# Batch 1's pooling in a fused attention and MoE kernel: plain loads and narrow matmuls in place of accumulating loads

## Chip, cores, metric

One core of one Trainium2 chip. The metric is device time in microseconds (us), the median of several executions. Ratios are the mean time of one kernel's fast runs over that of the other's fast runs of the same rounds, so they are not quite the ratio of the medians quoted beside them.

## What is computed

```python
# q: 4 x 12288 x 128   kv: 4 x 384 x 32 x 128   w_sr: 128 x 128
kv_pool = kv.reshape(B, H//4, 4, W//4, 4, C).mean(axis=(2, 4))    # 4 x 4 pixels -> 1: 768 rows a batch
k = v = kv_pool.reshape(B, -1, C) @ w_sr
a = softmax(q @ k.T / sqrt(C));  x = (a @ v).reshape(49152, 128)
h = x @ moe_w_in                                                  # 128 -> 2048
out = (h * sigmoid(1.702 * h)) @ moe_w_out                        # 2048 -> 128
```

## The kernel before

The work is cut into 96 groups of 512 queries; batch 1 begins at group 24. A **chunk** is 128 keys (attention) or 128 hidden units (MoE) for one group. A **tile** is up to three chunks: TensorE fills three PSUM banks (the fill), ScalarE (ACT) takes them in one activation and writes them to a ring of 108 chunk slots, and TensorE later uses each slot (12 value matmuls empty three attention chunks). Groups 0 to 47 go through attention, then through the MoE; then 48 to 95. A scheduler in the program places all this in one fixed order per engine. The parts that matter:

```python
def load_chunk(b, jc):              # batch 0 only: 1 MB of pixels, cast to bf16, into a free part of x
    a, ch = divmod(jc, HC)
    t = x_tile(XS - 1 - jc)
    nc.gpsimd.dma_start(out=t, in_=kv_r[b, a, ch])
    ...
def pool_chunk(b, jc):              # 16 matmuls of 32 columns sum the pixels
    ...
def add_kv(b, n):                   # batches 1 to 3: 16 loads, the later 14 ADD into what has landed
    i, w = divmod(n, r)
    if n == 0:
        kv_sums[b] = kvsum.tile([Hp, 2, Wp, C], F32, name="kvs")
    for i2 in range(2):
        nc.gpsimd.dma_start(out=kv_sums[b][:, i2], in_=kv_p[b, i, w, :, i2],
                            **({"accum_op": ADD} if n else {}))

def cast_q(s):                      # 2048 queries: f32 in DRAM -> bf16 in DRAM, GpSimd's queue
    nc.gpsimd.dma_start(out=q_bf[sl, :].rearrange("(p i) c -> p (i c)", p=128), in_=...)

def load_qT(s):                     # the same queries, transposed by the DMA, SP's queue
    qTs[s] = qpool.tile([128, 1, SG], BF, name="qT")            # three buffers
    nc.sync.dma_start_transpose(out=qTs[s], in_=q_bf[s * SG:(s + 1) * SG, :])

ADDS = [4, 6, 8, 9, 11, 12, 14, 15]
def background(i):                  # called when group i's first fill is placed
    s = i // 4
    if i % 4 == 0:
        if QS <= s + 2 < NS:
            load_qT(s + 2)          # first at i = 8: the queries of groups 16 to 19
        if CAST <= s + CAST < NS:
            cast_q(s + CAST)        # three tiles further ahead
    if i in ADDS:
        add_kv(1, ADDS.index(i))
    if i in (17, 19):
        use_kv(1, (i - 17) // 2)
    ...                             # i == 26 and 34: the two MoE weights
```

GpSimd's order of issue does not follow TensorE: it issues the next load as soon as that load's own waits are met. The queries of groups 0 to 15 are loaded directly and transposed on TensorE; the DMA transposes begin with those of group 16.

The softmax here doesn't subtract the row's maximum and nothing guards it: scores larger than these inputs give would overflow.

Of the kernel before, what the change touches and what calls it, by code (L numbers as in the profile page):

```python
# [20 lines left out]
def kernel(  # L21
    ctx, tc, q, kv, w_sr, moe_w_in, moe_w_out, out,
):
    nc = tc.nc
    B, N, C = q.shape
# [4 lines left out]
    JC = J // 128  # L30
# [9 lines left out]
    K = 3  # L40
# [37 lines left out]
    def acc(key=None):  # L78

        nonlocal last_acc  # L80
        last_acc = next_acc()
        if key:
            closes[last_acc] = key
        return banks[:, last_acc, :]

    def next_acc():
        return min((m for m in (13 - last_acc, last_acc) if m not in closes), key=lambda m: free[m])
# [12 lines left out]
    def x_tile(s):  # L100
        return x[:, s % XS * SG:(s % XS + 1) * SG]
# [5 lines left out]
    kv_tiles, kv_sums, pooled, pTs, kTs, vs = {}, {}, {}, {}, {}, {}  # L107

    def new_keys(b):
        kTs[b] = kvres.tile([128, J], BF, name="kT")  # L110

        vs[b] = kvres.tile([128, JC, C + 2], BF, name="v")
        nc.vector.memset(vs[b][:, :, C:C + 1], 1.0)

    def load_chunk(b, jc):
# [4 lines that stand above are left out]
        kv_tiles[b, jc] = t.rearrange("p (wp w1 c) -> p w1 wp c", w1=r, c=C)  # L120
# [19 lines left out]
    def value_chunk(b, jc):  # L140
        ps = acc()
        nc.tensor.matmul(ps[:, 0:128], pTs.pop((b, jc)), w_sr_sb, start=True, stop=True)
        nc.vector.tensor_copy(vs[b][:, jc, 0:C], ps[:, 0:128])


    def add_kv(b, n):
# [7 lines that stand above are left out]
    def sum_kv(b, a):  # L154
        t = kv_sums[b][:, :, 4 * a:4 * a + 4, :]
        pooled[b, a] = kvtmp.tile([Hp, 4, C], BF, name="pooled")
        nc.vector.tensor_tensor(pooled[b, a], t[:, 0], t[:, 1], ADD)  # L157
# [25 lines left out]
    def cast_q(s):  # L183
        sl = slice(s * SG, (s + 1) * SG)
        nc.gpsimd.dma_start(out=q_bf[sl, :].rearrange("(p i) c -> p (i c)", p=128),  # L185
                            in_=q_flat[sl, :].rearrange("(p i) c -> p (i c)", p=128))

    def load_qT(s):
        qTs[s] = qpool.tile([128, 1, SG], BF, name="qT")
        nc.sync.dma_start_transpose(out=qTs[s], in_=q_bf[s * SG:(s + 1) * SG, :])  # L190
# [58 lines left out]
    w_sr_sb = cpool.tile([128, C], BF)  # L249
# [46 lines left out]
    def room_ahead():  # L296
        busy = set(slot_of.values())
        return next((n for n in range(AG) if (head + n) % AG in busy), AG)
# [45 lines left out]
        nc.vector.tensor_copy(x[:, o:o + n * T], ps.rearrange("p k t -> p (k t)"))  # L344

    av_of, xt_of, turns = {}, {}, []
    ADDS = [4, 6, 8, 9, 11, 12, 14, 15]
    CAST = 5

    def background(i):  # L350
# [4 lines that stand above are left out]
                load_qT(s + 2)  # L355
            if CAST <= s + CAST < NS:
                cast_q(s + CAST)
        if i in ADDS:
            add_kv(1, ADDS.index(i))
        if i in (17, 19):  # L360
            use_kv(1, (i - 17) // 2)
        if i == 26:
            nc.gpsimd.dma_start(out=w_in_sb, in_=moe_w_in)
        if i == 34:
            nc.gpsimd.dma_start(out=w_out_sb, in_=moe_w_out.rearrange("(o p) c -> p o c", p=128))
# [9 lines left out]
    def use_kv(b, a):  # L375
        sum_kv(b, a)
        extras.extend([(transpose_pooled, b, a), (make_k, b, a), (make_v, b, a)])

    extras = []
# [55 lines left out]
    def prepare(p):  # L435
# [10 lines left out]
        for i, _ in part:  # L446
# [5 lines left out]
        0: [(pool_chunk, 0, 0), (warm, 2), (key_chunk, 0, 0), (warm, 2)],  # L452
        1: [(transpose_q, 1), (transpose_q, 2), (transpose_q, 3), (warm, 3)],
        2: [(pool_chunk, 0, 1), (value_chunk, 0, 0), (warm, 2), (key_chunk, 0, 1)],
        4: [(transpose_q, 4), (transpose_q, 5), (transpose_q, 6)],
        5: [(transpose_q, 7)],
        6: [(pool_chunk, 0, 2), (value_chunk, 0, 1)],
        8: [(key_chunk, 0, 2)],
        9: [(pool_chunk, 0, 3), (value_chunk, 0, 2)],
        11: [(key_chunk, 0, 3)],  # L460
        12: [(pool_chunk, 0, 4), (value_chunk, 0, 3)],
# [10 lines left out]

    FIXED, CHUNK, SWITCH, HANDOVER, EVACUATE, LATE = 0.33, 1.975, 6.0, 1.0, 4.5, 1.0
    COST = {pool_chunk: (2.5, 2.0), key_chunk: (0.7, 2.0), value_chunk: (0.7, 2.0),
            transpose_q: (1.2, 4.0),
            transpose_pooled: (1.5, 3.0), make_k: (1.0, 3.0), make_v: (1.5, 3.0), turn: (1.5, 3.5)}
    SMALL, TURN = 0.27, 5.5
    PAUSE = 4.0
    now, end, extra_at = 0.0, [], 0.0
    done = 0  # L480

    def fill(p):
        nonlocal now
        if p >= len(seq):
            return
        kind, part = seq[p]
        prepare(p)
        lo = K * (p % 2)
        (fill_attn if kind == "a" else fill_moe)(part, banks[:, lo:lo + len(part), :])
        if p >= 2:  # L490
            now = max(now, end[p - 2] + HANDOVER / 2)
        now += len(part)
        begin = max(now + HANDOVER / 2, end[p - 1] if p else 0.0)
        if p and kind != seq[p - 1][0]:
            begin += SWITCH
        end.append(begin + FIXED + CHUNK * len(part))
# [3 lines left out]
    for n in range(len(seq)):  # L500
        fill(n + 2)
        while True:
            room = room_ahead()
            limit = end[-1] - K - HANDOVER if n + 3 < len(seq) else 1e9
            bank = free[next_acc()]
            f = None
            if turns and max(now, bank) >= turns[0][0]:
                f, args = turn, turns[0][1:]
            if f is None and extras and now >= max(extra_at, bank):
                f, *args = extras[0]  # L510
            if f and max(now, bank) + COST[f][0] > limit + (LATE if f is turn else 3 * LATE) and room >= 4 * K:
                f = None
            if f:
                now = max(now, bank) + COST[f][0]
                f(*args)
                free[last_acc] = now + COST[f][1]
                extra_at = now + PAUSE
                if f is turn:
                    turns.pop(0)
                else:  # L520
                    extras.pop(0)
                continue
            if done == len(todo):
                break
            kind, i, c = todo[done]
            needs = at[("at" if kind == "a" else kind, i, c)]
            cost = K * SMALL if kind == "a" else 1.0
            if needs > n or (kind == "a" and i % TS == c == 0 and at["at", i + TS - 1, 1] > n):
                break
            start = max(now, end[needs] + HANDOVER)  # L530
            if c == 0 and (kind == "m" or i % TS == 0):
                start = max(start, bank)
            if start + cost > limit and not (room < 2 * K + 1 or (room < 4 * K and start == now)):
                break
            now = start + cost
            (drain_attn if kind == "a" else drain_moe)(i, c)
            done += 1
# [31 lines left out]
```

## Time and profile before

| | before |
|---|---|
| time, median (range) | 1021.14 us (1019.84 to 1021.26) |
| span in the profile | 1019.1 us |
| ACT busy; idle before softmax activations | 957.1 us (94%); 49.1 us |
| longest single wait of ACT | 36.0 us |

ACT is full from 104 us to the end. The lines, and how they are read, are in the prediction below.

### The profile page before, as it was taken

The numbers are of one execution on the slowest core, as the hardware profiler recorded it, in microseconds if no ns is written. First come the engines' busy times: TensorE is split into PE (matmuls) and PEld (weight loads), VectorE is DVE, ScalarE is ACT, GpSimd is POOL, SyncE is SP. The second block draws the span as 40 slices with busy tenths as digits, with TensorE's granted clock in tenths as the row PEclk, the third lists the DMA queues.
The fourth block names the chain that finished last, engine by engine and source line by source line (L and its number), as shares of the span: only waits on it lengthen the run. The fifth ranks groups of instructions, "written<-read, shape, count | busy, mean of one in ns | idle before, by whom it ended". The sixth has DMA issues, their size and how long they took to land.

```text
span 1019.1 us, 15867 instructions
## 1 busy us (share of the span) xinstructions
PE 961.4 (94%) x6461; PEld 525.2 (52%) x6579; DVE 228.1 (22%) x498; ACT 957.1 (94%) x713; POOL 79.3 (8%) x85
## 2 busy tenths in 40 slices
PE   7841999999999999999999999999999999999997
PEld 3530677774444444444445777775444444444443
DVE  4420444441111011101112444442011111011111
ACT  4950999999999999999999999999999999999996
POOL 4224123100023200000000000000000000000000
PEclk9985999999999999999999999999999999999999
DMA  9999999402269952222234121000222222222223
GB/s 181 194 139 149 189 161 159 55 2 32 42 102 159 185 103 39 34 41 42 42 57 79 42 63 42 2 2 11 42 42 42 38 36 41 42 42 42 39 36 50
DMA packets 284009, 72.42 MB, mean 71 GB/s; under 512 B 247712, under 2 KB 282144, under 8 KB 283616
## 3 DMA queue, kind: packets, MB, share of 16 engines
q0 software_dynamic: 39440, 35.66, 24.6%
q1 hardware_dynamic: 243440, 35.61, 22.2%
q8 instruction: 51, 0.84, 0.4%
q10 hardware_dynamic: 1056, 0.13, 0.1%
q14 instruction: 22, 0.18, 0.1%
HBM read 52.49 MB, written 35.65 MB: 86 GB/s over the span
## 4 chain that ended last, share of the span: by engine, by line
PE 85%; DMA 8%; ACT 3%; issue 2%; POOL 1%; DVE 1%; SPq 0%; POOLq 0%; DVEq 0%
PE banks L386 31%; PE banks L393 31%; PE banks L320 12%; PE banks L309 10%; DMA kvs<-in_kv_dram 6%; ACT ag L388 3%; PE banks L342 2%; DMA x<-in_kv_dram 2%; POOL kvs L151 0%; POOL x L197 0%; DMA out_dram<-o_sb 0%; POOL x L119 0%; DVE o_sb L400 0%; PE banks L162 0%; POOL q_bf L185 0%
## 5 line engine op out<-in xcount | busy, mean ns | idle before, releaser
L388 ACT ACTIVATE ag<-banks 128x1536 bf16<-128x1536 f32 x512 | 690.6, 1474 | 0.2
L386 PE MATMUL banks<-x,w_in_sb 128*128 128x512 bf16 x1489 | 412.4, 379 | 2.8 <-ACT ag L388 0.3
L393 PE MATMUL banks<-ag,w_out_sb 128*128 128x512 bf16 x1509 | 406.6, 379 | 1.4
L311 ACT ACTIVATE ag<-banks 128x1536 bf16<-128x1536 f32 (+2 forms) x196 | 260.7, 1457 | 49.1 <-PE banks L309 48.7
L393 PEld LDWEIGHTS <-w_out_sb 128*128 128x128 bf16 x1536 | 150.0, 98 | 179.3
L386 PEld LDWEIGHTS <-w_in_sb 128*128 128x128 bf16 x1536 | 147.7, 98 | 168.2 <-issue 2.3
L400 DVE STREAM_TRANSPOSE o_sb<-banks 128x512 f32<-128x512 f32 x96 | 68.7, 716 | 537.8 <-PE banks L393 509.2
L320 PEld LDWEIGHTS <-ag 128*128 128x128 bf16 x2304 | 152.2, 98 | 50.5 <-issue 2.3
L320 PE MATMUL banks<-v,ag 128*128 128x129 bf16 x2304 | 173.8, 220 | 0.3 <-DVE x L344 0.3
L309 PE MATMUL banks<-qT,kT 128*128 128x512 bf16 x532 | 154.7, 381 | 8.0 <-ACT ag L311 4.5
L151 POOL DMA_DIRECT2D kvs<-in_kv_dram x48 | 60.3, 1262 | 249.0 <-DMA kvs<-in_kv_dram 135.2
L331 DVE TENSOR_TENSOR xt<-banks,rec 128x384 bf16<-128x384 f32 x128 | 71.3, 557 | 4.4
L309 PEld LDWEIGHTS <-kT 128*128 128x128 bf16 x576 | 49.3, 97 | 34.5 <-issue 4.4
L344 DVE COPY x<-banks 128x768 bf16<-128x768 bf16 x64 | 35.6, 557 | 64.2 <-PE banks L342 64.2
L328 DVE RECIPROCAL rec<-banks 128x3 f32<-128x3 f32 x128 | 22.8, 178 | 97.4 <-PE banks L320 97.4
L162 PE MATMUL banks<-ident,pooled 96*128 96x96 bf16 x24 | 2.2, 217 | 35.6 <-DVE pooled L157 35.6
L342 PE MATMUL banks<-ident,xt 128*128 128x128 bf16 x384 | 31.8, 218 | 0.0
L342 PEld LDWEIGHTS <-xt 128*128 128x128 bf16 x384 | 24.8, 97 | 3.3
L162 PEld LDWEIGHTS <-pooled 96*128 96x128 bf16 x24 | 1.6, 102 | 37.3 <-DVE pooled L157 36.3
L185 POOL DMA_DIRECT2D q_bf<-in_q_dram x20 | 13.1, 912 | 11.9 <-DMA q_bf<-in_q_dram 5.3
L157 DVE TENSOR_TENSOR pooled<-kvs 96x512 bf16<-96x512 f32 x6 | 3.9, 658 | 35.0 <-DMA kvs<-in_kv_dram 35.0
L214 DVE COPY qT<-banks 128x512 bf16<-128x512 bf16 x15 | 9.8, 687 | 4.9 <-PE banks L208 4.8
(47 smaller groups left out, 72.5 us busy)
## 6 DMA issues: line engine op xcount, KB each, us to landing
out_dram<-o_sb SPq DMA_DIRECT2D x382, 64.0 KB, 2.0
kvs<-in_kv_dram POOLq DMA_DIRECT2D x48, 384.0 KB, 6.8
q_bf<-in_q_dram POOLq DMA_DIRECT2D x20, 512.0 KB, 18.0
x<-in_kv_dram POOLq DMA_DIRECT2D x6, 512.0 KB, 14.4
x<-in_q_dram POOLq DMA_DIRECT2D x3, 512.0 KB, 20.8
w_in_sb<-in_moe_w_in_dram POOLq DMA_DIRECT2D x1, 512.0 KB, 15.1
w_out_sb<-in_moe_w_out_dram POOLq DMA_DIRECT2D x1, 512.0 KB, 26.0
x<-in_q_dram POOLq DMA_DIRECT2D x1, 384.0 KB, 7.4
```

What stands on the lines that cost most here:

```text
L151: nc.gpsimd.dma_start(out=kv_sums[b][:, i2], in_=kv_p[b, i, w, :, i2], **({"accum_op": ADD} if n else {}))
L309: nc.tensor.matmul(ps[:, k, :], kTs[i // GB][:, jc * 128:(jc + 1) * 128], rhs, start=True, stop=True)
L311: nc.scalar.activation(place([("a",) + c for c in chunks]), ps, AF.Exp, scale=scale)
L320: nc.tensor.matmul(av_of[u][:, k * (C + 1):(k + 1) * (C + 1)], weights(("a", i, jc))[:, o:o + T], vs[i // GB][:, jc, 0:C + 1], start=(jc = ...
L328: nc.vector.reciprocal(rec, ps[:, :, C])
L331: nc.vector.tensor_tensor(xt_of[u // 2][:, u % 2 * TS:u % 2 * TS + TS, :], ps[:, :, 0:C], rec.unsqueeze(2).broadcast_to([128, TS, C]), MUL)
L342: nc.tensor.transpose(ps[:, k, :], xt[:, k, :], ident)
L344: nc.vector.tensor_copy(x[:, o:o + n * T], ps.rearrange("p k t -> p (k t)"))
L386: nc.tensor.matmul(ps[:, k, :], w_in_sb[:, fc * 128:(fc + 1) * 128], x[:, g % (4 * XS) * G:(g % (4 * XS) + 1) * G], start=True, stop=True)
L388: nc.scalar.activation(place([("m",) + c for c in chunks]), ps, AF.Gelu_apprx_sigmoid)
L393: nc.tensor.matmul(o_of[g], w_out_sb[:, fc, :], weights(("m", g, fc)), start=(fc == 0), stop=(fc == FCH - 1))
L400: nc.vector.transpose(o_sb, o_of.pop(g))
```

## The change

The intent: batch 1 no longer hangs on a chain of 16 loads each waiting for another. Its pixels are loaded by six plain loads at group 9, pooled by narrow matmuls as batch 0's are, and a chunk's key and value rows are made in one PSUM bank. The whole diff:

```diff
+    def key_and_value(b, jc):
+        if jc == 0:
+            new_keys(b)
+        ps = acc()
+        nc.tensor.matmul(ps[:, 0:128], w_sr_sb, pTs[b, jc], start=True, stop=True)
+        nc.tensor.matmul(ps[:, 128:256], pTs.pop((b, jc)), w_sr_sb, start=True, stop=True)
+        nc.vector.tensor_copy(kTs[b][:, jc * 128:jc * 128 + 128], ps[:, 0:128])
+        nc.vector.tensor_copy(vs[b][:, jc, 0:C], ps[:, 128:256])
@@
-    ADDS = [4, 6, 8, 9, 11, 12, 14, 15]
@@ background(i)
-        if i in ADDS:
-            add_kv(1, ADDS.index(i))
-        if i in (17, 19):
-            use_kv(1, (i - 17) // 2)
+        if i == 9:
+            for jc in range(JC):
+                load_chunk(1, jc)
+        if 0 <= i - 16 < JC:
+            extras.append((key_and_value, 1, i - 16))
+        if 0 <= i - 15 < JC:
+            extras.append((pool_chunk, 1, i - 15))
@@ scheduler
-            transpose_q: (1.2, 4.0),
+            transpose_q: (1.2, 4.0), key_and_value: (1.0, 3.0),
@@
-            if f and max(now, bank) + COST[f][0] > limit + (LATE if f is turn else 3 * LATE) and room >= 4 * K:
+            if f and max(now, bank) + COST[f][0] > limit + (LATE if f is turn else 4.5) and room >= 4 * K:
```

## The prediction

> **What bounds the kernel now.** I read the page first, for the engine that is busiest and the time at which it is not.
>
> ```profile
> PE   7841999999999999999999999999999999999997
> ACT  4950999999999999999999999999999999999996
> PEclk9985999999999999999999999999999999999999
> DMA  9999999402269952222234121000222222222223
> ...
> L388 ACT ACTIVATE ag<-banks 128x1536 bf16<-128x1536 f32 x512 | 690.6, 1474 | 0.2
> L311 ACT ACTIVATE ag<-banks 128x1536 bf16<-128x1536 f32 (+2 forms) x196 | 260.7, 1457 | 49.1 <-PE banks L309 48.7
> ```
>
> Each slice is 25.5 us. From the fifth on ScalarE (ACT) and TensorE (PE) are both full, and ACT's gate is exact: 0.2 us of idle time before 512 activations of the gelu, 49.1 us before the 196 of the softmax. So ACT sets the pace everywhere except in the first four slices, where the fourth digit is 0 on ACT and 1 on PE. The waits say what that hole is, and ACT's timeline says how long.
>
> ```profile
> ACT ag L311 <- PE banks L309: 48.7, 14, 36.0
> DVE pooled L157 <- DMA kvs<-in_kv_dram: 35.0, 1, 35.0
> PE banks L162 <- DVE pooled L157: 35.6, 2, 35.4
> POOL kvs L151 <- DMA kvs<-in_kv_dram: 135.2, 38, 20.6
> ```
>
> ```profile
> 39.35 25.63 ACT L311 ACTIVATE ag<-banks 128x1536 bf16<-128x1536 f32 x19 [1.44 <-PE banks L309]
> 100.95 1.45 ACT L311 ACTIVATE ag<-banks 128x1536 bf16<-128x1536 f32 x1 [35.97 <-PE banks L309]
> 103.59 7.12 ACT L311 ACTIVATE ag<-banks 128x1536 bf16<-128x1536 f32 x5 [1.19 <-PE banks L309]
> 110.90 20.47 ACT L311 ACTIVATE ag<-banks 128x1536 bf16<-128x1536 f32 x15 [0.19 <-PE banks L309]
> ```
>
> The longest wait of each line is one and the same event: ACT waits 36.0 us for scores, TensorE 35.4 us for batch 1's pooled rows, VectorE 35.0 us for the accumulating loads that make them. Nothing computes from 65 to 98 us. TensorE's queue is in order, so the transposes of batch 1's pooled rows, placed behind the fill of group 17, block scores that need nothing of batch 1. The chain of waits shows the loads as a serial line:
>
> ```profile
> 49.64 14.31 DMA kvs<-in_kv_dram
> 64.24 6.92 DMA kvs<-in_kv_dram
> 71.70 5.90 DMA kvs<-in_kv_dram
> 77.89 7.86 DMA kvs<-in_kv_dram
> 86.14 5.76 DMA kvs<-in_kv_dram
> 92.19 6.11 DMA kvs<-in_kv_dram
> ```
>
> One load of 384 KB is issued when the one before it into the same half has landed, 6 to 8 us a link, each behind whatever else is queued.
>
> **What the Trainium skill says.** "Perfetto Trace Analysis", Optimization Strategy: find the gaps on the engine that should be full, and what it waits for; that is the reading above, and the trace agrees (one gap of 36.0 us). "DMA: Bandwidth & Descriptors", Rules for kernel authors: an accumulating DMA reads its destination and writes it later, so the next one must wait for the earlier one's semaphore; the trace agrees, GpSimd waits 38 times, 135.2 us, for such loads. A plain load with cast has no such rule, so chunks can stand in the queue together. "TensorE: Matmul & The Clock Gate", Wait — 56ns, not 53.3ns?: starts come no closer than about 25 ns however narrow the matmul, and 55.6 ns apart at 128 columns. Here 16 pooling matmuls of 32 columns start at 19.36 us and the next instruction at 19.77, so 25.6 ns each, and 12 value matmuls of 129 columns take 0.69 us between two fills, 57.5 ns each. The same page, What's actually happening: an idle array drops to half clock and needs some 3.4 us of work to recover. The windows view gives a granted clock of 0.50 in 70 to 98 us, and the first fills after it take 1.48 us where they take 0.81.
>
> **Part by part.**
> The stall. Activations start every 25.63/19 = 1.349 us. The last of the 19 starts at 64.98 - 1.45 = 63.53 us. The one that starts at 110.90 is seven later, so without a stall it would start at 63.53 + 7 x 1.349 = 72.97 us. The stall with its clock recovery costs 110.90 - 72.97 = 37.9 us, all on the path.
>
> Do the new loads come in time? Loads of this queue are issued with eight in flight: an issue waits for the eighth before it. The gaps between those waits at the start are about 2.5 us, so one 512 KB load lands every 2.5 us. The third cast of queries to DRAM, issued at 17.64, lands near 38.3 (the cast group's early landings take 20.7 us), and the first accumulating load at 39.5. In the new order of issue the fourth cast takes that place, near 41, and the six chunks follow: 43.5 to 56 us. Transposed query loads run beside them from 36.55 us (their queue holds 45.7% of the DMA engines in 40 to 60 us); I allow two of some 5 us each. Estimate: first chunk at 48, last at 66 us. The tiles they overwrite held batch 0's chunks, and the last pooling read of those is at 30.7 us, so this holds nothing back. In the built order of instructions the first pooling stands behind the 33rd fill and the last behind the 45th. The 33rd fill ends near 59.3 in the trace of before, and 12 tiles later is 75.5. Margin about 10 us at both ends. No wait is expected.
>
> TensorE's work. Removed for batch 1: 8 transposes, 2 matmuls of 384 columns, 6 of 128, about 1.2 us. Added: 96 narrow matmuls at 25.6 ns = 2.5 us and 12 of 128 columns = 0.7 us. Net +2.0 us. A tile in that stretch holds 0.65 (fill) + 0.41 (pooling) + 0.17 (3 value matmuls) = 1.23 us, under 1.349, so ACT does not see it; the price is value matmuls put off. Counted in the built orders, the chunks filled but not yet used rise from 66.8 to 78 of 108 slots at tile 45 and from 84.8 to 96 at tile 93. Then the slots run out: in the changed order, tiles 115 to 127, already in the first gelu stage, hold bunches of 15, 18 and 21 value matmuls where before had at most 12. Summing 0.65 per fill, 0.058 per value matmul and 0.335 per turn over tiles 111 to 127 gives 24.8 us of TensorE, where ACT needs 17 x 1.348 = 22.9; less half a tile of lead, ACT loses about 1.4 us.
>
> The end. 26 instead of 23 output matmuls are left after the last fill; in before this tail keeps TensorE busy beyond ACT (23 from 1008.70, end 1013.83). Three more at 0.21 us: +0.6 us.
>
> VectorE trades 2 additions of 0.66 and 6 copies for 18 casts of 0.29 us; it is 22% busy, so beside other work. The later stretch has a DMA share no fuller than before's 110 to 180 us, in which ACT hardly waited.
>
> Sum: 1021.1 - 37.9 + 1.4 + 0.6 = 985.2 us; I say **985.5**.
>
> **The rivals.**
> A: the chunks come late and a shorter stall takes the stall's place. Against it, the 10 us margin, which is three or four landings; for it, DMA shares of 1.0 to 1.2 in 10 to 60 us, and transposes whose landing ranges from 3.8 to 15.6 us. If the queue were 10 us slower than I think, TensorE would wait a few us at the first or last chunk: 987 to 996.
> B: query transposes starve. Without the accumulating chain GpSimd no longer throttles itself, so casts, weights and batch 2's additions queue up at once, and the transposed loads share the engines. Each has some 8 groups x 2.7 us = 21.6 us from the issue to its use, more than the longest landing of 15.6. If one came late: 988 to 993.
> C: TensorE is the real bound, as busy as ACT at 94%, and the added work and the fuller slots eat more than I counted: each us of overrun in tiles 32 to 130 goes straight to ACT. All 2.0 us of extra work plus more jitter gives 987 to 989.
> D: the hole was only moved, for instance because batch 1 had to be waited for anyway. Batch 1's keys are first used at group 24, tile 52, near 86 us, later than all of the above. I give this 2%, at 1000 to 1020.
>
> **Range and chances.** Low end: no bunching loss and the full 37.9, with a little better start: 982. High end: half of A or all of C: 992. Faster by over 2% means below 1000.7; only D or a very bad A reaches it: faster 0.95, same 0.04, slower 0.01.
>
> **What would show it.** In the profile after, ACT's fourth slice should be 9, the softmax group's idle time about 12 to 14 us in place of 49.1, and the longest wait of ACT for scores under 4 us, that of the start. The weight loads of the pooling line should wait for chunks under 1 us in all. TensorE's clock should stay at 1.00 from 60 to 110 us. A few waits of ACT of 0.2 to 0.6 us near tiles 115 to 127, some 155 to 175 us, would show the bunching right; none, or more than 3 us, would show it wrong. A wait of the pooling matmuls for loads of kv of several us would mean A; fills waiting for transposed queries, B.

## The result, and the profile after

1005.56 us, median of 4 runs (1004.92 to 1007.97), beside 1020.49 us for the kernel before in the same rounds: ratio 0.9858, interval 0.9839 to 0.9878. The predicted gain was 35.6 us, the measured one some 15, and the 1.4% falls short of the "faster by over 2%" that was given a chance of 0.95.

The page after, the same rows as the prediction shows of before, then the two groups of activations:

```profile
PE   7849999999999999999999999999999999999997
ACT  4947999999999999999999999999999999999996
PEclk9988999999999999999999999999999999999999
DMA  9999992002299932222235231001222222222223
...
L399 ACT ACTIVATE ag<-banks 128x1536 bf16<-128x1536 f32 x512 | 691.3, 1470 | 1.0 <-PE banks L397 0.7
L320 ACT ACTIVATE ag<-banks 128x1536 bf16<-128x1536 f32 (+2 forms) x196 | 260.8, 1453 | 31.4 <-PE banks L318 31.2
```

The hole is still there. It is now in the third slice and the start of the fourth (4 and 7 on ACT), and the softmax's idle time fell from 49.1 to 31.4 us, not to the 12 to 14 foretold. The waits of the kernel after say what TensorE lacks now:

```profile
ACT ag L320 <- PE banks L318: 31.2, 17, 17.0
...
PEld L318 <- DMA qT<-q_bf: 16.9, 2, 16.6
PE banks L318 <- DMA qT<-q_bf: 16.6, 2, 16.4
```

Nothing of batch 1. The pooling's weight loads waited under 1 us for pixels, as foretold. What is late is a transposed query load. ACT's timeline after:

```profile
39.50 21.60 ACT L320 ACTIVATE ag<-banks 128x1536 bf16<-128x1536 f32 x16 [1.43 <-PE banks L318]
78.14 1.45 ACT L320 ACTIVATE ag<-banks 128x1536 bf16<-128x1536 f32 x1 [17.04 <-PE banks L318]
...
91.66 41.77 ACT L320 ACTIVATE ag<-banks 128x1536 bf16<-128x1536 f32 x31 [0.17 <-PE banks L318]
```

Groups 0 to 7 take the 20 early activations and each later group takes two. ACT stops 16 after the 20, so before the 37th, the first of group 16: the first group whose queries come by DMA transpose. The SP queue's timeline shows that load (start, then how long SP was held by it), first of the kernel before, then of the kernel after:

```profile
36.55 3.89 SPq L190 DMA_TRANSPOSE qT<-q_bf  x1
```

```profile
36.70 28.23 SPq L199 DMA_TRANSPOSE qT<-q_bf  x1
```

And the time of all 20 transposed loads from issue to landing (shortest, median, longest), before and after:

```profile
DMA to landing us min/median/max: 3.8/4.4/15.6
```

```profile
DMA to landing us min/median/max: 3.8/5.4/39.9
```

Issued within 0.2 us of the same moment, the first one landed 5.8 us later before, and 39.9 us later after. Where the time went, by stage, from ACT's timelines (the third column is experiment e1 below; the 1.3 us in which ACT loads its table before the first gelu stand in no row):

| stage | before | after | e1 |
|---|---|---|---|
| start to the 21st activation | 39.4 | 39.5 | 39.1 |
| the 80 activations from there to the first gelu (80 x 1.349 = 107.9 at full pace) | 146.3 | 128.1 | 108.8 |
| first gelu stage | 345.2 | 346.7 | 346.7 |
| second half, to ACT's last activation | 478.3 | 478.2 | 478.2 |
| tail | 8.7 | 9.3 | 9.3 |

Of the 38.4 us that the old stall cost, 20.2 came back as a new one: 17.0 us of waiting, and then refills at half clock (the windows view gives a granted clock of 0.50 in 75 to 80 us, and the first two fills take 1.46 and 1.49 us where they take 0.81).

### The profile page after: what moved, and what is told of

It is laid out like the page before. It is cut to its first block, busy times and chain, and to the rows that moved or that the text cites. A ratio compares the mean times of both kernels' runs of the same rounds, so it can differ in the third digit from the quotient of the medians.

```text
span 1003.1 us, 16170 instructions
## 1 busy us (share of the span) xinstructions
PE 970.1 (97%) x6671; PEld 527.4 (53%) x6671; DVE 229.1 (23%) x508; ACT 957.8 (95%) x713; POOL 62.3 (6%) x75
## 4 chain that ended last, share of the span: by engine, by line
PE 89%; ACT 5%; DMA 4%; DVE 1%; issue 1%; SPq 1%; POOL 0%; ACTq 0%; POOLq 0%
PE banks L397 31%; PE banks L404 31%; PE banks L329 13%; PE banks L318 11%; ACT ag L399 3%; DMA qT<-q_bf 3%; PE banks L351 2%; ACT ag L320 1%; DMA x<-in_q_dram 1%; DVE qT L223 1%; SPq L199 0%; PE banks L217 0%; DMA out_dram<-o_sb 0%; PE banks L128 0%; DVE o_sb L411 0%
## 5 line engine op out<-in xcount | busy, mean ns | idle before, releaser
L320 ACT ACTIVATE ag<-banks 128x1536 bf16<-128x1536 f32 (+2 forms) x196 | 260.8, 1453 | 31.4 <-PE banks L318 31.2
L318 PE MATMUL banks<-qT,kT 128*128 128x512 bf16 x576 | 157.8, 382 | 22.1 <-DMA qT<-q_bf 16.6
L160 POOL DMA_DIRECT2D kvs<-in_kv_dram x32 | 40.2, 1268 | 221.0 <-DVE pooled L166 131.0
L337 DVE RECIPROCAL rec<-banks 128x3 f32<-128x3 f32 x128 | 22.9, 179 | 99.9 <-PE banks L329 99.9
L351 PEld LDWEIGHTS <-xt 128*128 128x128 bf16 x384 | 24.8, 97 | 3.1
L194 POOL DMA_DIRECT2D q_bf<-in_q_dram x20 | 10.5, 696 | 26.0 <-DMA x<-in_kv_dram 14.1
L217 PE MATMUL banks<-ident,x 128*128 128x128 bf16 x64 | 5.8, 219 | 3.0 <-DVE qT L223 1.9
L128 PEld LDWEIGHTS <-x 128*128 128x128 bf16 x192 | 6.4, 97 | 2.1 <-DMA x<-in_kv_dram 0.6
L217 PEld LDWEIGHTS <-x 128*128 128x128 bf16 x64 | 4.3, 97 | 6.2 <-issue 3.3
```

Of the source, the lines that this page charges most:

```text
L318: nc.tensor.matmul(ps[:, k, :], kTs[i // GB][:, jc * 128:(jc + 1) * 128], rhs, start=True, stop=True)
L320: nc.scalar.activation(place([("a",) + c for c in chunks]), ps, AF.Exp, scale=scale)
L337: nc.vector.reciprocal(rec, ps[:, :, C])
L351: nc.tensor.transpose(ps[:, k, :], xt[:, k, :], ident)
```

## Why the load was late: the theories

Three, before the experiments. **Turns by packet** (mine): a DMA engine with two queues to serve takes one packet of each in turn, whatever their size. A transposed load is 2080 packets of about 256 bytes. Before, GpSimd waited 15.6 us for its own loads, until 40.05, so its queue ran nearly empty beside the first transposed load (218 packets from 36.5 to 42.5 us); the later ones stood beside accumulating loads in packets of about 500 bytes. After, GpSimd no longer waits for itself, so chunks (packets of 4 KB) and casts (larger still) stand in the queue without a gap. The Trainium skill has this rule: "DMA: Bandwidth & Descriptors", Queues, rings and completion order, says that each engine round-robins "at *packet* granularity". (It has a packet as typically 9 to 17 descriptors; whether the profile counts the same thing as a packet is not shown here.) I had not used it. **Shares by bytes**: the engines are simply full, and a load gets its part of the bytes. **The same tensor**: casts write the DRAM tensor that the transposed load reads.

The DMA view of 53 to 61 us (queue: packets, MB, share of the 16 engines' time; q1 is the transposed loads, q0 is GpSimd's), before, where these are the second and third of the loads, and after, where it is still the first:

```profile
q1 hardware_dynamic: 2006, 0.51, 95.3%
q0 software_dynamic: 721, 0.36, 57.7%
```

```profile
q0 software_dynamic: 176, 1.90, 111.4%
q1 hardware_dynamic: 172, 0.04, 3.7%
```

After, the two queues moved 176 and 172 packets, one for one, and 1.90 against 0.04 MB. From 61 to 69 us it was 208 and 208. GpSimd's mean of some 11 KB a packet hides what a cast looks like. From 58 to 62 us, where only casts moved in its queue, the view of after has

```profile
DMA packets 96, 0.80 MB, mean 200 GB/s; under 512 B 72, under 2 KB 72, under 8 KB 72
q0 software_dynamic: 48, 0.79, 91.5%
```

so 24 packets over 8 KB carry all of the 0.79 MB, some 33 KB each; the packed trace has each of them as 32,768 bytes that take 2.4 us. From 69 to 78 us GpSimd's packets are down to some 540 bytes on average (1831, 0.98 MB), the load's own are 1839, and it gets 0.46 MB and lands: one for one still, but a turn now costs little.

## Experiments

All are the changed kernel with the edit shown. They ran on several chips, each beside the kernel before, whose medians were 1020.45 to 1021.22 us. In short:

| run | time, us | first transposed load, issue to landing |
|---|---|---|
| after | 1005.56 | 39.9 |
| e1 every cast waits for a transposed load | 985.23 | 4.2 |
| e2 only casts 8 and later wait | 985.64 | 20.1 |
| e3 small rows in casts 8 and later, no wait | 986.34 | 24.3 |
| e4 casts 7 and later to another tensor | 1005.14 | 40.9 |
| e7 e2 with small rows in the chunks | 985.66 | 11.7 |

### e1: casts wait for transposed loads

```diff
+    gate = cpool.tile([128, 1], BF)
@@ background(i)
                 load_qT(s + 2)
+                nc.gpsimd.tensor_copy(gate, qTs[s + 2][:, 0, SG - 1:SG])
```

GpSimd reads one column of the landed tile, so whatever it issues next waits for that landing.

> The changed kernel, but GpSimd reads one column of each transposed query tile before it issues the cast of the same call, so that it cannot queue loads ahead of the first transposed load (that of group 16) and casts follow one for one. My theory, turns by packet: the 16 DMA engines take one packet of each queue in turn, and a transposed load of 256-byte packets beside loads of 4 KB and more gets a few per cent of the bytes. Then the first transposed load, alone but for two casts, lands within 10 us in place of 39.9, TensorE's wait for it goes, the chunks are still in time, and the time is 984 to 989 us (ratio to before 0.964 to 0.969). Rival, the same tensor in HBM is written by casts while it is read: the same gain. Rival, the stall of after has another cause than the queue of GpSimd's loads (the transposed load is slow in itself, or TensorE's added work): stays at 1000 to 1006.

985.23 us (984.96 to 985.44, 4 runs), ratio 0.9663 (0.9648 to 0.9678). The DMA view of e1 around the first transposed load, and e1's softmax group:

```profile
qT<-q_bf SPq DMA_TRANSPOSE x1, 4.2
```

```profile
L320 ACT ACTIVATE ag<-banks 128x1536 bf16<-128x1536 f32 (+2 forms) x196 | 260.3, 1456 | 11.8 <-PE banks L318 11.6
```

The stall is gone, and the 11.8 us that are left are those of the start. This kernel beats both. So the loads queued beside the transposed load caused the new stall; which property of them, e1 cannot say.

### e2: chunks may stand beside it, casts 8 and later may not

```diff
                 load_qT(s + 2)
+                if s > 2:
+                    nc.gpsimd.tensor_copy(gate, qTs[s + 1][:, 0, SG - 1:SG])
```

> The same gate, but only before casts 8 and later: cast 7 and the six chunks (packets of some 4 KB) stay free to queue beside the first transposed load, casts 8 and later wait for it. Turns by packet: it gets one packet of 256 bytes for one of 4 KB until the chunks have landed near 57 us, some 700 of its 2048 packets, and the rest in some 5 us: it lands near 61 to 63 us (25 us from issue), a stall of 0 to 4 us is left, time 985 to 991. Shares by bytes, or casts writing the tensor that it reads: the chunks hinder it little, it lands within 12 us, no stall, 984 to 987.

985.64 us (985.14 to 986.26), ratio 0.9666. The load took 20.1 us and was in time, some 5 us sooner than I had it. E2's DMA view of 45 to 53 us, while the chunks land:

```profile
q0 software_dynamic: 428, 1.56, 96.8%
q1 hardware_dynamic: 428, 0.11, 10.3%
```

One for one again, at 3.6 KB against 256 bytes. The chunks (with a few last packets of the casts before them) slow it from 4.2 to 20.1 us; it is the casts behind them that made it too late. The two rivals, which had it land within 12 us, fail here.

### e3: the same casts in small rows

```diff
     def cast_q(s):
+        if s >= 8:
+            nc.gpsimd.dma_start(out=q_bf[sl, :].rearrange("(i p) c -> p i c", p=128),
+                                in_=q_flat[sl, :].rearrange("(i p) c -> p i c", p=128))
+            return
```

> The changed kernel without any gate, but casts 8 and later are the same copy written as rows of 128 elements (256 bytes to DRAM) in place of long runs: the same bytes in the same order of issue, only smaller packets. Turns by packet: from about 57 us the first transposed load gets a packet for each packet of a cast of its own size and lands near 62 to 66 us in place of 76.6; the stall shrinks from 17 us to 2 to 6 us; time 988 to 996. Shares by bytes, a full engine, or writing the same tensor: the landing stays near 77 us or gets later, time 1004 to 1012, since small packets only cost.

986.34 us (985.75 to 987.03), ratio 0.9674. Nothing waits, the same bytes stand in the same queue, and yet the load lands 24.3 us after its issue instead of 39.9. E3's DMA view of 53 to 61 us, to be read against the one of after above:

```profile
q0 software_dynamic: 2212, 0.93, 92.8%
q1 hardware_dynamic: 1834, 0.46, 48.6%
```

With packets of a few hundred bytes beside it, it got 0.46 MB where it had 0.04. The stall left was 0.8 us, less than my 2 to 6, and the time below my 988 to 996. This is what tells packet size from volume.

### e4: casts to another tensor

```diff
+    q_bf2 = nc.dram_tensor("q_bf2", (B * N, C), BF, kind="Internal").ap()
@@ cast_q and load_qT
-        q_bf[...]
+        (q_bf if s < 7 else q_bf2)[...]
```

> The changed kernel, but casts 7 and later write a second DRAM tensor, so that nothing writes the tensor which the first three transposed loads read. Turns by packet: nothing changes, the first transposed load lands after 38 to 42 us, time 1004 to 1008. Rival, reads of a tensor under writing are slow: it lands within 15 us and the time falls to 984 to 990.

1005.14 us (1005.00 to 1005.38), and 40.9 us to landing: nothing changed. That casts write what is read plays no part.

### e7: the chunks in small rows as well

```diff
# on top of e2
+        if b == 1:
+            for o in range(2):                      # even pixels, odd pixels: rows of 256 bytes
+                nc.gpsimd.dma_start(out=t.rearrange("p (w o c) -> p o w c", o=2, c=C)[:, o],
+                                    in_=kv_r[b, a, ch].rearrange("p (w o c) -> p o w c", o=2, c=C)[:, o])
```

> As e2 (only casts 8 and later are gated), but each of batch 1's six chunks is loaded by two DMAs, its even and its odd pixels, so that a row that lands is 256 bytes in place of 4 KB. Same bytes, same place in the queue. In e2 the first transposed load took 20.1 us beside the 4 KB chunks. Turns by packet: beside packets of its own size it gets every second turn and the same bytes as its neighbour, so it lands within 8 to 13 us of its issue. Shares by bytes or by volume waiting in the queue: it stays near 20 us. Time: the chunks themselves come later (up to about 75 us), so 985 to 991.

985.66 us (985.14 to 991.13), ratio 0.967. The load took 11.7 us in place of e2's 20.1. The DMA view of 36.5 to 45 us, e2 (4 KB chunks) and e7:

```profile
q0 software_dynamic: 369, 1.41, 82.2%
q1 hardware_dynamic: 198, 0.05, 4.3%
```

```profile
q0 software_dynamic: 2866, 0.82, 90.8%
q1 hardware_dynamic: 1412, 0.36, 32.5%
```

The window includes a stretch before the load's packets reached the engines, but the share of bytes rose from 3% to 31%. It is no longer one packet for one, though: from 39 to 48 us, in which the whole load moved, GpSimd's queue moved 3976 packets to its 2080. So it got every third turn where I expected every second, and why stays open.

### e5: keys and values in two steps

```diff
# on top of e1
-            extras.append((key_and_value, 1, i - 16))
-            extras.append((pool_chunk, 1, i - 15))
+            extras.append((key_chunk, 1, i - 14)), extras.append((value_chunk, 1, i - 14))
+            extras.append((pool_chunk, 1, i - 13))     # conditions moved likewise
```

> As e1, but the keys and values of a chunk are made by two steps in two banks as before the change, and all steps are asked for two groups earlier (without that the check found keys read before they were written). If making both in one bank were what pays, this costs several us; I expect the two steps to cost only slightly more turns of a bank and fuller slots (81.75 of 108 chunks owed at tile 45 where e1 has 78): 985 to 988 us, at most 2 us more than e1's 985.2.

985.76 us (985.17 to 985.94), ratio 0.9658. That is 0.5 us more than e1, which ran on another chip, and by ratio 0.0005 less: no difference is shown. One bank for both pays little by itself. What it does is fit: with two steps asked for at the change's own groups, the check found keys read before they were written, and they had to start two groups earlier.

### e9 and e10: less and more pooling work

```diff
# on top of e1; e9 (wrong result on purpose), then e10; the scheduler's cost for the step adjusted
-            for w in range(r):
+            for w in range(r) if b == 0 else range(1):
+            for w in list(range(r)) * (1 + b):
```

> As e1, but with a wrong result on purpose: batch 1 is pooled from a quarter of its pixels, 4 narrow matmuls per chunk in place of 16, 1.8 us of TensorE work less before the slots run out. In the built order the bunches of 15 to 21 value matmuls begin at tile 118 instead of 112. My term for added TensorE work (slots fill, ACT loses what TensorE overruns): 0.7 to 1.6 us faster than e1, 983.6 to 984.5. Rival, TensorE has slack for it everywhere: the same as e1 within 0.4 us.

> As e1, but each chunk of batch 1 is pooled twice into the same bank (right result), 2.5 us of TensorE work more. Bunches begin at tile 106. My term: 1.5 to 2.8 us slower than e1, 986.7 to 988. Rival, slack everywhere: the same as e1 within 0.4 us.

983.99 us (983.46 to 984.58) and 987.69 us (987.25 to 988.07), in the same rounds: 3.7 us apart for 4.3 us of TensorE work. Against e1's 985.23 (another chip): 1.2 us faster for 1.8 us less of TensorE work, 2.5 us slower for 2.5 us more. e9's result was wrong as meant, e10's right. Added TensorE work in this stretch is largely paid for, though it stands beside a full ACT. But most of it is not paid where the prediction's term has it. By ACT's timelines the 80 activations before the first gelu took 108.3 us in e9, 108.8 in e1 and 110.9 in e10, and the first gelu stage 346.0, 346.7 and 347.1. So 2.1 us of e10's cost fell beside the pooling itself:

```profile
66.28 1.45 ACT L320 ACTIVATE ag<-banks 128x1536 bf16<-128x1536 f32 x1 [0.37 <-PE banks L318]
...
71.58 9.73 ACT L320 ACTIVATE ag<-banks 128x1536 bf16<-128x1536 f32 x7 [0.71 <-PE banks L318]
```

With the pooling doubled, a tile by the prediction's figures holds 0.65 + 0.82 + 0.17 = 1.64 us of TensorE, more than ACT's 1.349. That e10 hit its range is in part luck. What speaks for the slots is the 0.7 us of e9 and the 0.4 us of e10 in the gelu stage. How they cost ACT there, the kernel after shows, in TensorE's and ACT's timeline:

```profile
190.14 1.03 PE L329 MATMUL banks<-v,ag 128*128 128x129 bf16 x15
...
192.81 1.39 PE L329 MATMUL banks<-v,ag 128*128 128x129 bf16 x21
...
194.94 5.64 ACT L399 ACTIVATE ag<-banks 128x1536 bf16<-128x1536 f32 x4 [0.23 <-PE banks L397]
```

A bunch of 21 value matmuls delays the next fill, and ACT waits 0.23 us for it. There are three such waits. The rest of the stage's extra 1.5 us is ACT starting a little later each time.

### e11: only the first wait

```diff
# on top of e1
+                if s == 2:
                     nc.gpsimd.tensor_copy(gate, qTs[s + 2][:, 0, SG - 1:SG])
```

> As e1, but only the first gate is kept: cast 7 and the chunks wait for the first transposed load, every later cast is free to queue. Turns by packet: the first transposed load lands within 6 us as in e1, but the second (queries of group 20, issued near 47 us, used by the 45th fill near 74 us) now stands beside chunks, seven casts of large packets and the weights, some 45 us of transfers from 41 us on; it lands near 84 to 90 us. The stall moves from group 16 to group 20, 10 to 16 us of ACT, and the time is 996 to 1003 us. Rival, the first transposed load is special (it is the first of its queue, or follows the query tiles made by TensorE): no stall, 984 to 988.

1018.6 us (1015.38 to 1025.86), ratio 0.9973: a miss on the size. ACT's timeline of e11, taken in the slowest of the four runs:

```profile
87.82 1.45 ACT L320 ACTIVATE ag<-banks 128x1536 bf16<-128x1536 f32 x1 [15.65 <-PE banks L318]
...
120.62 1.45 ACT L320 ACTIVATE ag<-banks 128x1536 bf16<-128x1536 f32 x1 [20.62 <-PE banks L318]
```

The first stall came where and as large as foretold: group 20, 15.65 us, its load 37.8 us on the way. So no transposed load is special, and one wait only moves the stall. But a second stall of 20.62 us followed at group 24, whose load took 41.8 us. Its cause differs. From 100 to 110 us, e11's DMA view gives

```profile
q1 hardware_dynamic: 538, 0.14, 84.0%
```

that is some 250 ns of engine time a packet on average (84% of 16 engines' 10 us over 538), where e1's first transposed load alone took 20 ns a packet (58.3% of 16 x 4.4 us over 2080), and GpSimd's queue moved only 0.48 MB in those 10 us. This is not a matter of turns.

### e12: batch 2's loads out of the way

```diff
# on top of e11, background_moe(g)
+        if g == 2:
+            nc.gpsimd.tensor_copy(gate, qTs[13][:, 0, SG - 1:SG])
```

> As e11, but the loads of batch 2 also wait, for the last transposed load of this stage. In e11 the stall at group 20 came as expected, 15.7 us, but a second one of 20.6 us at group 24 did not: between 90 and 117 us the transposed loads' packets took some ten times as long each, while the first two loads of batch 2 stood in the same queue. If those loads are what slows them, the second stall goes and the time is 998 to 1004. If it is the state of that chip's memory in those executions, or the casts still in the queue, the time stays at 1010 to 1026.

1015.92 us (1009.76 to 1018.84), ratio 0.9947, interval 0.988 to 1.0014. The second stall was 13.28 us where e11, in its slowest run, had 20.62, but it stayed, with batch 2's loads out of the queue. So they are at most part of it. What was left in the queue were casts from DRAM to DRAM and the last of the second MoE weight, which took 46.8 us to land in e11 and 36.6 in e12. Why packets took so long beside them stays open, and so do the spreads of 10 us among e11's and 9 us among e12's runs. Neither touches the change itself: in the kernel after the queue beside the load moved 1.55 to 1.90 MB in each 8 us from 45 to 69 us, and the load's own packets took no more than some 30 ns each (3.7% of 16 x 8 us over 172, and likewise in the other two windows). They were short, and waited.

## Why the prediction was wrong

The step that failed is rival B, "query transposes starve", and in it this: "Each has some 8 groups x 2.7 us = 21.6 us from the issue to its use, more than the longest landing of 15.6." It took the longest landing in before as a bound for after. A landing time belongs to its neighbours: 4.2 us nearly alone, 11.7 beside small rows, 20.1 beside the chunks, 39.9 beside chunks and casts. In the sum itself the transposed loads stand only as a delay of the chunks ("I allow two of some 5 us each"), never as something that the chunks delay. A share of busy time does not say who gets it: 95.3% of the engines' time was q1's in one window of before and 3.7% in the same window of after. The prediction did see what set this off ("GpSimd no longer throttles itself, so casts, weights and batch 2's additions queue up at once") and then priced it at 3 to 8 us. It was 20.2.

The other steps, one by one:
- **The old stall, 37.9 us**: right. e1 has it gone and gains 37.5 us in that stage.
- **Chunks in time, no wait**: right; under 1 us. They landed at most 20.5 us after their issue, the last of which was at 35.6, so by some 56 us where the prediction had 66; the first is read at 59.4.
- **TensorE's work, +1.4 us**: right in size; the first gelu stage grew by 1.5 us in after and in e1. Two slips in the working: 24.8 - 22.9 less half a tile is 1.2, not 1.4, and tiles 115 to 127 lie at some 169 to 187 us without the stall, not 155 to 175 (e1's gelu begins with tile 100 at 149.17). The three waits came at tiles 119, 125 and 131. That full slots are the path is shown in part (e9 and e10).
- **The tail, +0.6 us**: right; 8.7 to 9.3 us.
- **The sum**, 985.2: what the change is worth once the transposed loads are served; e1 measured 985.23, and its stages agree with the terms within half a us, so this is not luck.
- Rivals A and C did not happen. D, "the hole was only moved", at 1000 to 1020 us, has the number right, but for another cause than the one it gave: batch 1 was not waited for. TensorE's clock did not stay at 1.00 from 60 to 110 us, since the stall was still there.

The accumulating chain had a second effect, which rival B named and underrated. By waiting for itself it held GpSimd's queue short, and that kept the transposed loads fast. Taking the chain out took the brake out with it.

## What to carry to other kernels

Before removing a wait on a queue, ask what else that wait held back, and who shares the engines with what is now let through. Where a DMA of small packets (a transpose) shares engines with queued DMAs of large packets, expect turns by packet and estimate its share from the two sizes (one for one in most windows here, one for two in e7); then order the large ones behind its landing, each time and not only once, or cut their rows small. The time to landing of a transfer can be taken over into a prediction only if its neighbours stay the same.

## What the Trainium skill lacked or had wrong

- "DMA: Bandwidth & Descriptors", Queues, rings and completion order: the rule of turns by packet is there and held in most windows (176 to 172, 208 to 208, 428 to 428 packets), but not beside e7's small rows (3976 to 2080). What it lacks is the consequence for a DMA transpose: its packets are about 256 bytes, so it got 0.04 MB where its neighbour moved 1.90 MB.
- The same page, SWDGE vs HWDGE vs iDMA, has packets of at most 4096 bytes preferably. The DRAM-to-DRAM casts here came to some 33 KB a packet in the profile (0.79 MB in 24, from 58 to 62 us), and they are the worst neighbours: 0.04 MB of the load in 8 us beside casts, 0.11 beside chunks.
- The same page, Latency and other measured facts, gives a DMA transpose 261 GB/s, or 350 to 400 when contiguous. Here one of 512 KB took 4.2 us almost alone, some 125 GB/s from issue to landing (while its packets moved, e1's view of 36.2 to 40.6 us shows some 290 GB/s, so the figure itself is not contradicted), and 39.9 us, some 13 GB/s, beside queued loads, of which the figure says nothing.
- The same page, Rules for kernel authors, advises to issue a DMA early and wait late. Here loads issued early, some of them tens of us before their use, cost 17 us at another load's wait; no page has a caution.
- No page has what made packets of a transposed load take some 250 ns each beside a few DRAM-to-DRAM casts and other late loads (e11), and no run here settles it.
